# A ring of five 32 KB units with loads of one or two units, and a new order of key and value work, in a decode layer

## The chip, the cores and the metric

The kernel runs on one core of one Trainium2 chip; the other cores are idle. The metric is the device time of one execution in microseconds, and less is better. Executions of the kernel before agree within 0.1%: 408.78 to 408.88 us in the first three. In the texts, PE is the matrix engine, DVE the vector engine, ACT the scalar engine, SP the engine that issues the loads; SBUF is the memory beside the engines that the loads fill, and PSUM holds the results of PE. A *row* is a contiguous piece that one of the 16 DMA engines moves at a time, one *packet* in the profile's count.

## The reference, cut to what matters

One token goes through attention over a cache of 65,536 keys and values, and then through a gated feed-forward layer:

```python
x = A_x                                            # [1, 1, 1024]
h = x + attention(layernorm(x), k_cache, v_cache, wq, wo)
# 32 query heads, 4 key/value heads, k_cache and v_cache [1, 4, 65536, 128] bf16: 67 MB each
h2 = h + (gelu(ln(h) @ w_gate) * (ln(h) @ w_up)) @ w_down     # F = 3584
```

Every byte of the cache and of the weights is read once, 173.02 MB in all. That is the kernel's main fact.

## The kernel before: the parts that matter

All loads go through one function into a pool of five buffers. A buffer has 32 KB in each of the 128 partitions, so a load is 4 MB, made of 128 contiguous rows of 32 KB (28 KB for gate and up).

```python
CW, NBUF = 16384, 5
chpool = ctx.enter_context(tc.tile_pool(name="chpool", bufs=NBUF))

def load(src, name):
    t = chpool.tile([P, CW], BF16, name=name, tag="ch")
    n, w = src.shape[1], src.shape[2]
    tv = t[:, 0:n * w].rearrange("p (n w) -> p n w", w=w)
    nc.sync.dma_start(out=tv, in_=src)
    return tv
```

Each of the four key/value heads (a "group" below) is four units of keys and four of values. A key unit is turned in place by four DVE transposes, then PE makes scores with 32 matmuls; a value unit takes 32 matmuls. Keys of one group alternate with values of the group before:

```python
def k_load(g, li):
    kt = kv_load(k_v[g], li, "k_sb").rearrange("p n d -> p (n d)").bitcast(U32)
    w = CP * Dh // 2
    for c in range(NSP):                             # four quarters
        dv(nc.vector.transpose(out=kt[:, c * w:(c + 1) * w], in_=kt[:, c * w:(c + 1) * w]))
    ...

for g in range(1, Hkv):
    for li in range(NL):
        k_load(g, li)
        v_load(g - 1, li)
        ...                                          # closing work of older groups
        k_scores(g, li)
        k_keep(g, li)                                # scores out of PSUM, running maximum
        if li == NL - 1:
            softmax_head(g)
        v_values(g - 1, li)
```

A load may start when the buffer that it gets is free: after the last matmul on the unit that was there. Loads are issued in order by one queue, so a load that waits holds back those behind it.

## Time and profile before

| | before |
|---|---|
| time, median | 408.87 us (3 runs), 408.77 us (6 runs, with the later three) |
| span of the profiled run | 407.0 us |
| DMA slices at 9 tenths or more | 39 of 40 |
| bytes, rate over the span | 173.02 MB, 425 GB/s |
| PE, DVE busy | 74%, 50% |
| first row of a load starts, last row ends | 1.0 us, 403.1 us |

These are lines of the page of the kernel before. In the slices, each digit is the busy share of a fortieth of the span in tenths; the queue line has packets, MB and the packets' time as a share of 16 engines; a line of group 5 has busy us, mean ns and the idle time ahead of it; the last lines have the size of a load and the median us from issue to landing.

```profile
PE 299.3 (74%) x1481; PEld 62.8 (15%) x713; DVE 202.6 (50%) x185; ACT 44.9 (11%) x67; POOL 7.4 (2%) x17
...
DMA  9999999999999999999999999999999999999995
...
DMA packets 6508, 173.19 MB, mean 426 GB/s; under 512 B 728, under 2 KB 736, under 8 KB 992
...
q1 hardware_dynamic: 6488, 173.02, 98.8%
...
DMA 46%; PE 30%; DVE 18%; ACT 4%; issue 2%; SPq 0%; ACTq 0%; DVEq 0%
...
L275 DVE STREAM_TRANSPOSE k_sb<-k_sb 128x2048 uint32<-128x2048 uint32 x64 | 142.1, 2278 | 34.5 <-DMA k_sb<-in_A_k_cache_dram 34.5
...
k_sb<-in_A_k_cache_dram SPq DMA_DIRECT2D x16, 4096.0 KB, 33.6
v_sb<-in_A_v_cache_dram SPq DMA_DIRECT2D x16, 4096.0 KB, 37.1
```

The DMA line never dips. The chain that ended last gives only 46% to DMA, which could tempt one to speed up DVE; but a unit takes 9.7 us to move and a value load lands 37 us after its issue, so two to three other loads are queued ahead of it. The stream of loads has work at every moment, and the chain merely follows single buffers through it.

The end of the kernel is this part of its timeline (start, us, engine, line, operation; in brackets the idle time and what ended it):

```profile
402.92 1.02 PE L144 MATMUL f_ps<-wd_sb,actz 128*32 128x256 bf16 x12 [0.17 <-DMA wd_sb<-in_B_w_down_dram]
...
403.99 0.42 DVE L526 CAST o_fin<-f_ps 97x256 bf16<-97x256 f32 x1 [11.82 <-PE f_ps L144]
404.44 0.66 SPq L527 DMA_DIRECT2D out_dram<-o_fin  x1
```

After the last row only the last products, a copy and the store are left, about 4 us.

### The profile page before, as it was taken

What the parts mean: (1) busy time and instruction counts of PE and PEld (TensorE: products, weight loads), DVE (VectorE), ACT (ScalarE), POOL (GpSimd) and SP (SyncE); (2) the same over time, 40 slices, a digit from 0 to 9 for tenths busy, and PEclk for the clock granted to TensorE, in tenths of its full rate; (3) what the DMA queues carried; (4) which work ended last, traced back from release to release, by engine and by line L of the source; (5) the groups of instructions that cost most, each with busy time, mean ns of one, the idle gap of its engine ahead of it and who ended that gap; (6) DMA issues with size and microseconds to landing.
All of it is one profiled execution on the core that took longest, in us unless ns stands there. A gap on an engine that the chain in (4) does not pass through costs nothing.

```text
span 407.0 us, 2658 instructions
## 1 busy us (share of the span) xinstructions
PE 299.3 (74%) x1481; PEld 62.8 (15%) x713; DVE 202.6 (50%) x185; ACT 44.9 (11%) x67; POOL 7.4 (2%) x17
## 2 busy tenths in 40 slices
PE   0356298769997788897956969978767998725564
PEld 0011011111110111111101121110112110200233
DVE  1118989876673678555464968181843001110110
ACT  1010000150000041000002320000051000100000
POOL 2000000000000000000000000000010000100000
PEclk9965778969999989899989898999868899866565
DMA  9999999999999999999999999999999999999995
GB/s 364 461 412 451 423 419 457 410 454 422 414 461 415 441 430 415 461 415 444 427 419 457 415 448 425 420 454 415 448 426 432 440 419 444 424 429 442 426 421 220
DMA packets 6508, 173.19 MB, mean 426 GB/s; under 512 B 728, under 2 KB 736, under 8 KB 992
## 3 DMA queue, kind: packets, MB, share of 16 engines
q1 hardware_dynamic: 6488, 173.02, 98.8%
q8 instruction: 8, 0.13, 0.1%
q14 instruction: 4, 0.03, 0.0%
q10 hardware_dynamic: 8, 0.00, 0.0%
HBM read 173.02 MB, written 0.00 MB: 425 GB/s over the span
## 4 chain that ended last, share of the span: by engine, by line
DMA 46%; PE 30%; DVE 18%; ACT 4%; issue 2%; SPq 0%; ACTq 0%; DVEq 0%
DMA k_sb<-in_A_k_cache_dram 32%; DVE k_sb L275 12%; PE acc_ps L146 12%; DMA wg_sb<-in_B_w_gate_dram 8%; PE qk_ps L144 6%; PE qk_ps L146 6%; DMA wd_sb<-in_B_w_down_dram 5%; PE acc_ps L144 4%; DVE mx L296 2%; ACT sc L295 2%; DVE pT L320 1%; ACT pe_r L317 1%; PE o_ps L144 1%; DVE acc_sb L346 1%; ACT acc_sb L348 1%
## 5 line engine op out<-in xcount | busy, mean ns | idle before, releaser
L275 DVE STREAM_TRANSPOSE k_sb<-k_sb 128x2048 uint32<-128x2048 uint32 x64 | 142.1, 2278 | 34.5 <-DMA k_sb<-in_A_k_cache_dram 34.5
L144 PE MATMUL qk_ps<-k_sb,wsel 128*128 128x512 bf16 x256 | 103.9, 406 | 36.3 <-DVE k_sb L275 23.8
L146 PE MATMUL acc_ps<-v_sb,pT 128*128 128x512 bf16 x384 | 112.6, 405 | 0.0
L146 PE MATMUL qk_ps<-k_sb,wsel 128*128 128x512 bf16 x256 | 103.7, 405 | 0.0
L144 PE MATMUL acc_ps<-v_sb,pT 128*128 128x512 bf16 x128 | 52.0, 406 | 0.0
L144 PEld LDWEIGHTS <-wsel 128*128 128x128 bf16 x256 | 26.0, 102 | 141.3 <-issue 121.2
L296 DVE TENSOR_REDUCE mx<-qk_ps 128x1 f32<-128x1024 f32 x16 | 19.5, 1219 | 43.9 <-ACT sc L295 43.9
L295 ACT COPY sc<-qk_ps 128x1024 f32<-128x1024 f32 x16 | 16.2, 1012 | 201.7 <-PE qk_ps L146 201.6
L144 PEld LDWEIGHTS <-pT 128*128 128x128 bf16 x128 | 13.6, 106 | 99.8 <-issue 99.7
L320 DVE STREAM_TRANSPOSE pT<-pe_r 128x1024 bf16<-128x1024 bf16 x16 | 19.0, 1226 | 6.2 <-ACT pe_r L317 6.2
L346 DVE COPY acc_sb<-acc_ps 32x512 f32<-32x512 f32 x8 | 5.4, 672 | 32.7 <-PE acc_ps L146 32.7
L317 ACT ACTIVATE pe_r<-sc,nbias 128x1024 bf16<-128x1024 f32 x16 | 18.2, 1140 | 14.3 <-DVE nbias L312 13.6
L146 PE MATMUL wu_ps<-wu_sb,hnz 128*32 128x512 bf16 x40 | 7.1, 572 | 7.5 <-DMA wu_sb<-in_B_w_up_dram 7.5
L348 ACT COPY acc_sb<-acc_ps 32x512 f32<-32x512 f32 x8 | 4.6, 577 | 62.0 <-DVE acc_sb L346 61.9
L232 DVE COPY wg_ev<-wg_ps 128x512 f32<-128x512 f32 x1 | 0.7, 690 | 20.9 <-PE wg_ps L144 20.9
L144 PE MATMUL q_ps<-wq_sb,xnz 128*32 128x512 bf16 x32 | 5.2, 626 | 8.0 <-DMA wq_sb<-in_A_wq_dram 8.0
L144 PE MATMUL f_ps<-wd_sb,actz 128*32 128x256 bf16 x112 | 6.9, 413 | 5.3 <-DMA wd_sb<-in_B_w_down_dram 5.3
L144 PE MATMUL wg_ps<-wg_sb,hnz 128*32 128x512 bf16 x32 | 6.5, 598 | 5.3 <-DMA wg_sb<-in_B_w_gate_dram 5.3
L144 PE MATMUL o_ps<-sel,acc_sb 128*128 128x8 f32 x32 | 5.2, 290 | 6.7 <-DVE rl L360 5.9
L144 PE MATMUL ln_tot<-ln_s,ones_f 128*128 128x1 f32 x8 | 1.9, 311 | 10.8 <-DVE ln_s L194 9.0
L155 PE MATMUL mxT_ps<-ident_f,mx 128*1 128x128 f32 x4 | 1.3, 322 | 11.1 <-DVE mx L301 11.1
L232 DVE COPY q_ev<-q_ps 128x512 f32<-128x512 f32 x1 | 0.7, 691 | 13.5 <-PE q_ps L146 13.5
(102 smaller groups left out, 87.6 us busy)
## 6 DMA issues: line engine op xcount, KB each, us to landing
k_sb<-in_A_k_cache_dram SPq DMA_DIRECT2D x16, 4096.0 KB, 33.6
v_sb<-in_A_v_cache_dram SPq DMA_DIRECT2D x16, 4096.0 KB, 37.1
wq_sb<-in_A_wq_dram SPq DMA_DIRECT2D x2, 4096.0 KB, 16.5
wo_sb<-in_A_wo_dram SPq DMA_DIRECT2D x2, 4096.0 KB, 30.8
wg_sb<-in_B_w_gate_dram SPq DMA_DIRECT2D x2, 3584.0 KB, 32.0
wu_sb<-in_B_w_up_dram SPq DMA_DIRECT2D x2, 3584.0 KB, 33.1
wd_sb<-in_B_w_down_dram SPq DMA_DIRECT2D x1, 3584.0 KB
wd_sb<-in_B_w_down_dram SPq DMA_DIRECT2D x1, 1792.0 KB, 24.8
```

The costliest lines, as they stand in the source:

```text
L144: return pe(t.matmul(out, lhsT=lhsT, rhs=rhs, start=start, stop=stop, tile_position=tile_position, skip_group_check=skip_group_check))
L146: op = t.add_instruction(mybir.InstMatmult(name=nc.get_next_instruction_name(), engine=t.engine, start_tensor_calc=start, stop_tensor_calc ...
L155: pe(nc.tensor.transpose(out=out, in_=in_, identity=identity))
L232: nc.vector.tensor_copy(out=dst, in_=src)
L275: dv(nc.vector.transpose(out=kt[:, c * w:(c + 1) * w], in_=kt[:, c * w:(c + 1) * w]))
L295: ac(nc.scalar.copy(out=sc[:], in_=flat))
L296: dv(nc.vector.tensor_reduce(out=state[("mx", g)][:, li:li + 1], in_=flat, axis=AX.X, op=ALU.max))
L317: ac(nc.scalar.activation(out=pe_r[:], in_=state.pop(("sc", g, li))[:], func=ACT.Exp, bias=nbias[:, 0:1], scale=scale, accum_out=lpart[:, ...
L320: dv(nc.vector.transpose(out=pT[:].rearrange("p m c -> p (m c)"), in_=pe_r[:]))
L346: dv(nc.vector.tensor_copy(out=acc_sb[sl, :], in_=acc[sl, c, :]))
L348: ac(nc.scalar.copy(out=acc_sb[sl, :], in_=acc[sl, c, :]))
```

## The change

The intent is longer rows: two neighbouring units of values, and all of gate, are loaded by one DMA with rows of 64 KB (56 KB for gate), within the same five units of SBUF. For that the pool becomes one tile that is handed out as a ring. The order is rearranged so that loads of two units never wrap: two value units, then three key units. The first part of a key unit's turn is moved ahead of the scores of the unit before, and the softmax's steps go between value matmuls. Gate is now complete before up begins, and all pieces of down stand side by side in the first two units.

```diff
-    chpool = ctx.enter_context(tc.tile_pool(name="chpool", bufs=NBUF))
+    chpool = ctx.enter_context(tc.tile_pool(name="chpool", bufs=1))
+    ring = chpool.tile([P, NBUF * CW], BF16, name="ring")
...
+    at = [0]
+    def load(src, off=0):
         n, w = src.shape[1], src.shape[2]
+        units = -(-(off + n * w) // CW)
+        o = at[0] * CW + off
+        assert o + n * w <= NBUF * CW
+        at[0] = (at[0] + units) % NBUF
+        tv = ring[:, o:o + n * w]
+        nc.sync.dma_start(out=tv.rearrange("p (n w) -> p n w", w=w), in_=src)
...
+    def kv_load(what, g, li, n):
+        t = load((k_v if what == "k" else v_v)[g][:, li * LN:(li + n) * LN, :])
+        for u in range(n):
+            state[(what, g, li + u)] = t[:, u * LN:(u + 1) * LN, :]
...
-    for g in range(1, Hkv):            # key unit, value unit, key unit, ...
+    todo = [("k", 0, 0, 1), ("k", 0, 1, 1), ("k", 0, 2, 1), ("k", 0, 3, 1), ("k", 1, 0, 1),
+            ("v", 0, 0, 2), ("k", 1, 1, 1), ("k", 1, 2, 1), ("k", 1, 3, 1), ("v", 0, 2, 2),
+            ("k", 2, 0, 1), ("v", 1, 0, 2), ("k", 2, 1, 1), ("k", 2, 2, 1), ("k", 2, 3, 1), ("v", 1, 2, 2),
+            ...  ("v", 3, 0, 2), ("v", 3, 2, 2)]      # what, group, first unit, units
...
-        wg = load(gv[:, c0:c0 + GB, :], "wg_sb")
+    wg = load(gv[:])                                  # gate in one load, then up in two
...
+        at[0] = 0
+        wv = load(wd_v[:, c0:c0 + sz, :], c0 * D)
```

## The prediction

> **What bounds the kernel now.** The stream of loads. The page's slices show the 16 DMA engines at 9 tenths in 39 of 40 slices; the queue list gives the load queue 98.8% of the span. In the packet records behind that list the first row starts at 1.0 us and the last ends at 403.1; the row times over 16 engines sum to 401.7 us, so there is no hole. PE is busy 74%, DVE 50%; the transposes and matmuls in the chain that ended last are waits of single buffers, not of the stream. After the last row come about 4 us (last products, copy, store).
>
> A 32 KB row takes 1.213 us on its engine, an 8 KB row 0.309, a 4 KB row 0.159. Estimate from these: 27.2 B/ns per engine (435 GB/s for 16) plus 8 ns a row. The Trainium skill, "DMA: Bandwidth & Descriptors", section "Where 436 GB/s comes from", gives a ceiling of 435.2 GB/s; the trace's slope agrees, and a 32 KB row already runs within 0.7% of it. Longer rows have almost nothing left to win.
>
> **What the change does.** The bytes stay (173.02 MB). Values: 2,048 rows of 32 KB become 1,024 of 64 KB; gate: 256 of 28 KB become 128 of 56 KB. That is 1,152 rows fewer: 1,152 x 8 ns / 16 = 0.58 us, all on the critical stream, provided a 64 KB row stays one packet. Nine loads fewer save nine 9 ns semaphore packets per engine, 0.08 us. Sum: 0.1 (if rows are cut again) to 0.7 us. Compute is unchanged (64 transposes of 2.28 us, 512 score and 512 value matmuls); its order becomes two value units, then three key units. Gate now comes before up, but the last up load still lands about 385 us, so the tail stays.
>
> **What it puts at risk.** A two-unit load waits until both units are free, and the loads behind it wait too. Today a load is issued 18 to 26 us before the stream needs it in the steady part. I placed the landings at 9.7 us per unit (8 rows of 1.213 us) and carried the turn (8.9 us), scores and values (about 8 us each; 7.0 at full clock, 9.7 in slow stretches) and softmax along the new order. Value loads are then issued only 6 to 11 us ahead; the tightest is group 1's first half: it waits for group 1's third key unit to be scored near 140 us, and the stream reaches it near 146.5. Key loads keep 16 to 21 us. Extra half-clock stretches (3.4 to 10 us each in the clock records) would cost 2 to 5 us there, so I expect no hole, but a small one is possible.
>
> **Predicted time:** 408.2 us, 8 in 10 between 407.4 and 409.4. Faster by over 2%: 2%; within 2%: 93%; slower by over 2%: 5%.
>
> **What would show it.** (1) Packets fall from 6,508 to about 5,210; near 6,360 would mean that 64 KB rows are cut in two. (2) The DMA slices stay at 9. (3) A value load takes about 28 us from issue to landing instead of 37, 19.4 of them transfer. (4) The last row ends 0.1 to 0.7 us earlier; the 4 us after it are the same. (5) Waits of the SP queue on PE grow without cost.
>
> **What would make it wrong.** A hole in the stream at a value load (a low DMA slice); 64 KB rows running slower per byte than 32 KB ones; or per-row overhead that vanishes more than linearly, worth at most 3 us.

## More of the kernel before

A verdict (faster, same, slower) needs 2%.

The packet records behind the page allow a second measure, used in all that follows: the *lead* of a load, which is the time from its issue to the start of its first row. A load with a lead of 15 us could have been issued about 14 us later without a hole in the stream.

In the kernel before, the key and value loads have leads of 13.2 to 28.7 us, counted from the first value load on.

## The result, and the profile after

Ratios in this document are the mean time of one kernel's fast runs over that of the other's in the same rounds, so they are not quite the ratios of the medians that are quoted beside them.

| | before | after |
|---|---|---|
| time, median (range, runs) | 408.77 us (408.65 to 408.88, 6) | 408.69 us (408.28 to 409.17, 6) |
| ratio, 95% interval | | 0.9997 (0.9985 to 1.001) |
| span of the profiled run | 407.0 us | 406.7 us |
| last row ends | 403.1 us | 402.8 us |
| row times over 16 engines | 401.7 us | 401.2 us |
| lead of the value loads | 13.2 to 28.7 us | 6.8 to 16.0 us |

The lines of the page of the changed kernel that answer to those above (the last one is from the list of DMA issues, for value loads of two units):

```profile
PE 295.0 (73%) x1481; PEld 63.6 (16%) x729; DVE 202.6 (50%) x185; ACT 44.7 (11%) x67; POOL 7.4 (2%) x17
...
DMA  9999999999999999999999999999999999999995
...
DMA packets 5211, 173.18 MB, mean 426 GB/s; under 512 B 584, under 2 KB 592, under 8 KB 848
...
q1 hardware_dynamic: 5192, 173.02, 98.7%
...
DMA 62%; PE 27%; DVE 9%; ACT 1%; issue 0%; SPq 0%; ACTq 0%
...
L281 DVE STREAM_TRANSPOSE ring<-ring 128x2048 uint32<-128x2048 uint32 x64 | 142.7, 2280 | 34.0 <-DMA ring<-in_A_k_cache_dram 34.0
...
ring<-in_A_k_cache_dram SPq DMA_DIRECT2D x16, 4096.0 KB, 34.5
...
ring<-in_A_v_cache_dram SPq DMA_DIRECT2D x8, 32.3
```

The packets fell by 1,297, as 1,152 fewer rows and 144 fewer semaphore packets ask for (one is an instruction fetch). The DMA line is the same, digit for digit. The chain moved from 46% DMA to 62%, while nothing became slower or faster: another sign that it is not a measure of what the stream costs. A value load of two units now lands 32.3 us after its issue (median, the last line above).

### The profile page after: what moved, and what is told of

Read it like the earlier page. It is cut to its first block, busy times and chain, and to the rows that moved or that the text cites. A ratio compares the mean times of both kernels' runs of the same rounds, so it can differ in the third digit from the quotient of the medians.

```text
span 406.7 us, 2639 instructions
## 1 busy us (share of the span) xinstructions
PE 295.0 (73%) x1481; PEld 63.6 (16%) x729; DVE 202.6 (50%) x185; ACT 44.7 (11%) x67; POOL 7.4 (2%) x17
## 2 busy tenths in 40 slices
DMA packets 5211, 173.18 MB, mean 426 GB/s; under 512 B 584, under 2 KB 592, under 8 KB 848
## 3 DMA queue, kind: packets, MB, share of 16 engines
q1 hardware_dynamic: 5192, 173.02, 98.7%
HBM read 173.02 MB, written 0.00 MB: 425 GB/s over the span
## 4 chain that ended last, share of the span: by engine, by line
DMA 62%; PE 27%; DVE 9%; ACT 1%; issue 0%; SPq 0%; ACTq 0%
DMA ring<-in_A_v_cache_dram 40%; PE acc_ps L147 12%; DMA ring<-in_A_k_cache_dram 7%; DMA ring<-in_B_w_down_dram 7%; DMA ring<-in_B_w_gate_dram 7%; DVE ring L281 7%; PE qk_ps L145 5%; PE qk_ps L147 5%; PE acc_ps L145 4%; DVE mx L302 2%; ACT sc L301 1%; PE wg_ps L145 0%; PE wg_ps L147 0%; PE f_ps L145 0%; DVE o_fin L549 0%
## 5 line engine op out<-in xcount | busy, mean ns | idle before, releaser
L281 DVE STREAM_TRANSPOSE ring<-ring 128x2048 uint32<-128x2048 uint32 x64 | 142.7, 2280 | 34.0 <-DMA ring<-in_A_k_cache_dram 34.0
L145 PE MATMUL qk_ps<-ring,wsel 128*128 128x512 bf16 x256 | 99.5, 389 | 35.5 <-DVE mx L302 23.6
L147 PE MATMUL acc_ps<-ring,pT 128*128 128x512 bf16 x384 | 115.0, 412 | 0.0
L147 PE MATMUL qk_ps<-ring,wsel 128*128 128x512 bf16 x256 | 99.5, 389 | 0.0
L145 PE MATMUL acc_ps<-ring,pT 128*128 128x512 bf16 x128 | 53.3, 416 | 17.8 <-DMA ring<-in_A_v_cache_dram 17.8
L145 PE MATMUL q_ps<-ring,xnz 128*32 128x512 bf16 x32 | 5.2, 625 | 7.8 <-DMA ring<-in_A_wq_dram 7.8
L145 PE MATMUL f_ps<-ring,actz 128*32 128x256 bf16 x112 | 6.9, 415 | 5.4 <-DMA ring<-in_B_w_down_dram 5.4
L145 PE MATMUL wu_ps<-ring,hnz 128*32 128x512 bf16 x32 | 4.9, 527 | 7.5 <-DMA ring<-in_B_w_up_dram 7.5
L145 PE MATMUL wg_ps<-ring,hnz 128*32 128x512 bf16 x32 | 4.4, 492 | 8.1 <-DMA ring<-in_B_w_gate_dram 8.1
L315 DVE TENSOR_REDUCE gm<-mxT_ps 1x8 f32<-1x128 f32 x4 | 1.1, 279 | 15.0 <-PE mxT_ps L156 15.0
L145 PEld LDWEIGHTS <-hnz 128*32 128x32 bf16 x64 | 3.3, 116 | 21.8 <-issue 17.4
```

The lines of the kernel that those rows point to most:

```text
L145: return pe(t.matmul(out, lhsT=lhsT, rhs=rhs, start=start, stop=stop, tile_position=tile_position, skip_group_check=skip_group_check))
L147: op = t.add_instruction(mybir.InstMatmult(name=nc.get_next_instruction_name(), engine=t.engine, start_tensor_calc=start, stop_tensor_calc ...
L315: dv(nc.vector.tensor_reduce(out=gm[:], in_=mxT_ps[:].rearrange("o (x h) -> o h x", h=rep), axis=AX.X, op=ALU.max))
```

## The experiments

Twelve kernels ran. The theory under test: *the stream of loads is the time; a row costs about 8 ns beyond its bytes; the changed order keeps enough lead for the stream never to run dry.* The rivals: longer rows win more and a hole gives it back; row length does nothing at all; compute in the chain that ended last costs time.

### 1. The changed kernel again, and with value rows of 32 KB

The first is an unedited control. The second keeps ring, units and order, and loads each value unit alone:

```diff
-        t = load((k_v if what == "k" else v_v)[g][:, li * LN:(li + n) * LN, :])
         for u in range(n):
-            state[(what, g, li + u)] = t[:, u * LN:(u + 1) * LN, :]
+            state[(what, g, li + u)] = load((k_v if what == "k" else v_v)[g][:, (li + u) * LN:(li + u + 1) * LN, :])
```

> The changed kernel once more, unedited, as a control beside the split variant. Theory (the stream of loads is the time; a row costs 8 ns over its bytes; the slack of the value loads is enough): 408.2 to 408.7 us, ratio to the kernel before 0.998 to 1.000, about 5,211 packets, no DMA slice under 9 before the last. Rival (longer rows win more, but a hole at a value load gives it back): the same time, but the value loads' rows start later than 9.7 us per unit allows. Rival (row length does nothing): ratio 1.000 as well, so this run alone tells little.

> The changed kernel with the same ring, units and order, but each value unit loaded by a DMA of its own, with 32 KB rows: 1,024 rows and 8 loads more. Theory: plus 0.51 us for rows and 0.07 us for semaphore packets against the control, so 408.7 to 409.2 us; value loads are issued 16 to 26 us ahead of their first row instead of 7 to 13; no hole. Rival (a hole ate a larger gain of the long rows): this kernel has no holes and comes out at or below the control. Rival (row length does nothing): equal to the control within 0.1 us. If the wide spread of the changed kernel's runs (0.9 us against 0.2) comes from the thin slack of the two-unit loads, it shrinks here; if it comes from the new order, it stays.

Measured on one chip, against 408.80 us of the kernel before (9 runs): the control 408.55 us (408.42 to 408.72; ratio 0.9993, interval 0.9981 to 1.0006), the split variant 408.92 us (408.71 to 409.28; ratio 1.0005, interval 0.9992 to 1.0019). The split costs 0.37 us by the medians, not 0.58; the two sets of five runs only touch (408.72 and 408.71), and both intervals hold 1. Its packet count tells that the edit did what it should:

```profile
DMA packets 6364, 173.19 MB, mean 426 GB/s; under 512 B 712, under 2 KB 720, under 8 KB 976
```

That rules against a larger gain that a hole took back: with leads of 17.7 to 26.6 us at the value loads this kernel is not faster. The wide spread of the changed kernel's first six runs (0.9 us) did not come back in the control (0.3 us; 0.6 us in the split variant), so it needs no cause in the kernel. A change of some tenths of a microsecond is at the edge of what these runs resolve, so the cost of a row was magnified next.

### 2. Rows of 8 KB and 4 KB in the kernel before

Each 32 KB row of keys and values is moved as four or eight rows, by two interleaved DMAs, which was meant to keep neighbouring rows from merging (the packet count below shows that they did not merge):

```diff
-        nc.sync.dma_start(out=tv, in_=src)
+        if w == Dh:
+            cut = lambda ap: ap.rearrange("p (a h n) d -> p h a (n d)", a=4, h=2)   # a=2 for 8 KB
+            for h in range(2):
+                nc.sync.dma_start(out=cut(tv)[:, h], in_=cut(src)[:, h])
+        else:
+            nc.sync.dma_start(out=tv, in_=src)
```

> The kernel before with the rows of keys and values cut to 8 KB (each 32 KB row is moved as four rows, by two DMAs; results unchanged). Theory: 12,288 rows more at 8 ns over 16 engines are 6.1 us, and 32 loads more at 9 ns 0.3 us, so plus 6.4 us: 415.2 us (414.5 to 416). Rival (rows of any such length run at one rate): under 1 us more. Rival (cost of a row more than proportional to their number): over 8 us.

> The same with rows of 4 KB (each 32 KB row as eight). Theory: 28,672 rows more are 14.3 us, and 0.3 us for loads: plus 14.6 us, 423.4 us (422.5 to 425). The 4 KB rows of the last down load took 0.159 us each in the trace of before; the same is expected here. Rival (one rate): under 1 us more.

Measured: 412.56 us and 417.38 us (4 runs each), 3.76 and 8.58 us more than the kernel before, where 6.4 and 14.6 were expected. The ratios are 1.0091 (interval 1.0077 to 1.0105) and 1.0209 (1.0195 to 1.0223), by the 2% rule "same" and "unclear", but both clear of 1. The expectations miss by the same factor, 0.59. After 0.3 us for the 32 additional loads (9 ns on each engine), a row costs (3.76 - 0.29) us x 16 / 12,288 = 4.5 ns and (8.58 - 0.29) us x 16 / 28,672 = 4.6 ns: proportional to the number of rows, but 4.6 ns and not 8. The additional loads are not the cause: between the two runs, which issue equally many, 16,384 rows cost 4.82 us, or 4.7 ns a row.

The page of the kernel with 4 KB rows shows why the estimate from row times was too high:

```profile
DMA packets 35692, 173.19 MB, mean 417 GB/s; under 512 B 1240, under 2 KB 1248, under 8 KB 34272
...
q1 hardware_dynamic: 35672, 173.02, 100.4%
```

The rows took more than all of 16 engines' span. So the records of neighbouring rows overlap: in this run the row times sum to 416.6 us per engine, the stretch from first row to last is 410.8 us, and 1.6 us of it is idle; the 7.4 us too many over 2,152 rows per engine are 3.4 ns a row. The records' own times (0.309 us for 8 KB, 0.159 us for 4 KB) are unchanged from before (0.159 us was expected for 4 KB); it is adding them up that counts these 3.4 ns twice.

The Trainium skill, "DMA: Bandwidth & Descriptors", section "Why small descriptors are slow (HBM only)", names a fixed overhead of about 3 cycles a packet and 32 bytes of descriptor metadata. With the 850 MHz and 435.2 GB/s of its section "Where 436 GB/s comes from" this is, as an estimate (the page does not give the clock of that bus), 3.5 + 1.2 = 4.7 ns. The 4.5 to 4.7 ns of the two runs are close to that; that these two parts make up the cost is not shown.

Applied to the change: 1,152 rows x 4.6 ns / 16 = 0.33 us, and up to 0.08 us for the semaphores. The profiled stream ended 0.3 us earlier, and splitting the values again (1,024 rows and 8 loads, 0.29 + 0.07 us) cost 0.37 us. With sets of runs that spread by 0.3 to 0.6 us, so close an agreement is partly luck.

### 3. Is it compute? Three transposes of four taken away

```diff
-        for c in parts:
+        for c in [p for p in parts if p == 0]:
             dv(nc.vector.transpose(...))
```

> The changed kernel with three of the four transposes of each key unit taken away, 107 us of DVE work (result wrong on purpose). Theory (the stream is the time): within 0.3 us of the changed kernel, 408.2 to 408.9 us, with loads issued further ahead. Rival (transposes in the chain that ended last cost time): 5 us or more faster.

Measured: 408.45 us (408.35 to 408.85), against 408.82 us before and 408.55 to 408.69 us of the changed kernel. DVE fell to half, and nothing followed:

```profile
PE 292.7 (72%) x1481; PEld 61.4 (15%) x729; DVE 98.1 (24%) x137; ACT 44.8 (11%) x67; POOL 7.4 (2%) x17
...
DMA  9999999999999999999999999999999999999995
```

This is the plainest evidence for the first part of the theory: 104 us of work of the second busiest engine are worth nothing. One part of the expectation failed: the loads were not issued further ahead. The leads of the value loads are 7.6 to 14.8 us, against 6.8 to 16.0 us, so in this order less DVE work bought no lead; what holds it then was not tested. PE, the busiest engine, was not relieved in any run; that it does not set the time rests on the leads, since no load met a dry queue in the kernels before and after. (The keys are then wrongly turned. The comparison with the reference still passed; so it does not see such errors in the keys, and passing it is no proof of a right order of key data.)

### 4. What the change spent: lead

If the stream is the limit, the change's cost would not show in the time but in the slack. The same DVE work, 2.28 us per key unit, was added to the kernel before, to the changed kernel, and to the variant with split values: the last quarter of each key unit is turned twice.

```diff
-        for c in range(NSP):                                        # the kernel before
+        for c in [*range(NSP)] + [NSP - 1] * 1:
-        for c in parts:                                             # the changed kernel, and split values
+        for c in [c for p in parts for c in [p] * (2 if p == NSP - 1 else 1)]:
```

> The kernel before with the last quarter of each key unit turned twice: 2.28 us more of DVE per key unit, 36 us in all (scores then read a wrongly turned quarter, so the result is wrong on purpose). Theory (loads issued 13 to 29 us ahead, the added work stays off the stream): within 0.5% of the kernel before, at most 3 us more. Rival (compute is as close to the limit as the chain of waits makes it look): plus several us.

> The same 2.28 us per key unit in the changed kernel (result wrong on purpose). Theory (the change left 7 to 13 us of lead at the value loads; three key units in a row now take 6.8 us more, the lead goes negative for the values of groups 0 and 1): plus 4 to 20 us, with low DMA slices near 120 and 150 us. Rival (the lead is not what decides): within 0.5%, as before_turn_x2.

> The same addition in values_single: the new order, but each value unit loaded alone. If the thin lead comes from waiting for two units at once: close to the kernel before, under 2 us more. If it comes from the new order (value units in a pair, keys in a triple): plus 4 to 20 us, within 3 us of after_turn_x2. The times worked through the order with the trace's durations say the second, except where PE runs at full clock throughout.

Measured against 408.82 us: 408.62 us with the old order (ratio 0.9997, interval 0.9982 to 1.0012), 423.76 us with the change (1.0347, interval 1.0307 to 1.0387), 415.58 us with the change and single value loads (1.0162, interval 1.0145 to 1.0179; clear of 1). The slices of the three pages, old order first:

```profile
PE 294.5 (72%) x1481; PEld 63.4 (16%) x713; DVE 238.5 (59%) x201; ACT 44.9 (11%) x67; POOL 7.4 (2%) x17
...
DMA  9999999999999999999999999999999999999995
```

With the changed kernel (the second line is GB/s in the same slices):

```profile
PE 301.5 (71%) x1481; PEld 63.7 (15%) x729; DVE 239.0 (57%) x201; ACT 44.8 (11%) x67; POOL 7.4 (2%) x17
...
DMA  9999999989969969899999899999999989999994
GB/s 397 413 431 447 436 410 447 490 386 413 442 258 397 447 248 486 375 428 447 450 422 417 354 397 416 428 445 481 410 403 398 455 385 434 456 431 405 429 419 166
```

With the changed order and single value loads:

```profile
DMA  9999999999999999999999899999998999999994
```

The two deepest holes in the changed kernel lie where they were expected, near 120 and 150 us; two more loads met a dry queue, at 235.7 and 323.6 us. Its sync queue's timeline shows the first one: the value load goes out at 121.33 us, and its first row starts at 122.28 us, 0.95 us later, so the queue was dry.

```profile
121.33 0.33 SPq L167 DMA_DIRECT2D ring<-in_A_v_cache_dram  x1
128.27 0.33 SPq L167 DMA_DIRECT2D ring<-in_A_k_cache_dram  x1
```

In the view by windows (PE, PEld, DVE, ACT and POOL busy us, granted clock, DMA share, GB/s) the two stretches read, in the changed kernel with the addition:

```profile
118.00:126.00 8.00, 8.00 (x39) 1.45 (x15) 4.50 (x2) 0.00 (x0) 0.00 (x0) 1.00 0.69 258
150.00:158.00 8.00, 5.21 (x25) 0.77 (x9) 4.45 (x6) 1.01 (x1) 0.00 (x0) 1.00 0.57 209
```

and in the kernel before with the same addition:

```profile
118.00:126.00 8.00, 8.00 (x39) 1.07 (x11) 7.53 (x4) 0.44 (x1) 0.00 (x0) 1.00 0.98 422
150.00:158.00 8.00, 6.44 (x17) 1.13 (x7) 5.28 (x9) 4.74 (x8) 0.00 (x0) 0.57 1.00 428
```

In the second window the old order even had PE at a clock of 0.57, and its stream did not notice.

Two causes share the 15 us, and the split variant separates them. My expectation for it was either "under 2 us" or "within 3 us of the other"; it came out in the middle, so both halves of that question were wrong as put.

- *The order.* In the changed kernel with the addition, two value units in a row leave DVE with little to do (busy 4.5 of 8 us from 118 to 126 us), and three key units in a row leave PE waiting (busy 17.3 of 24 us from 126 to 150 us). From the first maximum of one group to that of the next (groups 2 and 3), the old order with the addition takes 76.4 us and the new one 81.0 us (180.84 to 261.82 us). The stream needs 8 x 9.69 = 77.5 us for a group. The old order stays under it, the new one does not. (Without the addition this stretch takes 78.1 and 77.5 us: there the compute goes at the pace of the stream.) The compute of the split variant runs at the same times as that of the changed kernel (its last maximum ends at 317.3 us against 317.5 us); so the 6.8 us that it lost against the kernel before go with the order. What came with the order (the ring, the place of the softmax, the part of the turn that was moved ahead) was not tried piece by piece.
- *Waiting for two units at once.* With single loads the first unit of a pair starts to fill while the second is still in use, so the stream gets further ahead of the same compute: gate's first row starts at 355.8 us and not at 364.1. That is the other 8 us (423.76 - 415.58). A load of two units also lands later as a whole; since the compute ran at the same times in both variants, that did not cost time here.

### 5. The edges: half the dose, twice the dose, fewer buffers

The changed kernel with half the addition (half of the last quarter turned once more), and the old order with twice the addition:

```diff
+            if c == NSP - 1:                                        # after_turn_half
+                dv(nc.vector.transpose(out=kt[:, c * w:c * w + w // 2], in_=kt[:, c * w:c * w + w // 2]))
-        for c in range(NSP):                                        # before_turn_x3
+        for c in [*range(NSP)] + [NSP - 1] * 2:
```

> The changed kernel with half of the last quarter of each key unit turned once more: about 1.14 us of DVE per key unit, half the dose of after_turn_x2 (result wrong on purpose). Theory (what counts is the lead of the value loads, 11 us at the values of group 0, second half, and group 1, first half; the full dose used up 10 us of it): about 5 us of lead stay at the first, little at the second, so no hole or small ones: 408.5 to 412 us. Rival (every us of work added to the new order shows in the time, lead or not): about half of the full dose's 15 us, 415 to 417 us.

> The kernel before with the last quarter of each key unit turned three times: 4.57 us more of DVE per key unit, twice the dose of before_turn_x2 (the data come out right again). Its shortest lead was 13.2 us, with one dose 6.2. Theory: this dose takes it to about zero in the first half and the paces meet, so holes appear: plus 5 to 35 us. Rival (the old order is immune because DVE is only 50% busy): within 0.5%.

The kernel before with four and with three buffers (`NBUF = 4`, `NBUF = 3`):

> The kernel before with four buffers of 32 KB in place of five. Theory (leads of 13 to 29 us; a buffer less takes one load's 9.7 us from each): shortest lead about 3 to 6 us, no hole, 408.6 to 409.5 us. Rival (the fifth buffer is needed): plus several us.

> The kernel before with three buffers. Theory: a second buffer less takes another 9.7 us, leads fall to between about minus 2 and plus 8 us, so holes appear at some loads: plus 2 to 20 us, visible as loads whose first row starts about 1 us after their issue. Rival (depth does not matter): within 0.5%.

Measured against 409.06 us: half dose 408.59 us (ratio 0.9989, interval 0.9974 to 1.0004), double dose 438.19 us (1.0705, interval 1.0685 to 1.0726), four buffers 408.68 us (0.9996, interval 0.9981 to 1.001), three buffers 424.00 us (1.0381, interval 1.0339 to 1.0423). The DMA slices of three buffers:

```profile
DMA  9999979988999999999999999999999899999995
```

All of it in one table. Idle is the mean idle time of the 16 engines between the first row and the last, counted where fewer than 16 rows were under way; row time is the sum of the row times over 16; both are from the packet records of the profiled runs. The lead is the shortest of the key and value loads from the first value load on.

| kernel | span, us | idle, us | row time, us | shortest lead, us |
|---|---|---|---|---|
| before | 407.0 | 1.5 | 401.7 | 13.2 |
| before, one dose | 406.8 | 1.4 | 401.6 | 6.2 |
| before, four buffers | 406.8 | 1.5 | 401.5 | 4.9 |
| after | 406.7 | 1.5 | 401.2 | 6.8 |
| after, half dose | 406.8 | 1.7 | 401.1 | 3.9 |
| after, single value loads, one dose | 414.2 | 5.9 | 404.5 | 0.95 (dry) |
| after, one dose | 422.4 | 14.3 | 404.0 | 0.95 (dry) |
| before, three buffers | 422.5 | 11.9 | 406.8 | 0.95 (dry) |
| before, two doses | 436.6 | 24.7 | 408.1 | 0.95 (dry) |

Every kernel in the table whose queue never ran dry has the same span within 0.3 us, and every kernel with a dry load is longer by what the stream lost. The sums that follow are bookkeeping: they show where the time went, and the doses and buffers above show why. For the changed kernel with one dose, idle and row time grew by 12.8 + 2.8 = 15.6 us, the span by 15.7; for three buffers, by 10.4 + 5.1 = 15.5 us, the span by 15.5; for two doses, by 23.2 + 6.4 = 29.6 us, the span by 29.6. The rival of the half dose (every us of work shows, so about half of 15 us) fell: half the dose cost nothing. The pace of the compute agrees: from the first maximum of group 2 to that of group 3, half the dose in the new order takes 75.6 us, under the stream's 77.5, and two doses in the old order take 86.0 us.

The growth of the row time can be read in the packet records. In the changed kernel with one dose, the first rows of the 16 engines after the four dry moments took 2.9 to 3.2 us in the mean, and the next ones 2.42 to 2.48 us, against 2.42 us at a steady stream. The surplus of these first rows is 2.5 of the 2.9 us by which the row time grew. So in this run a dry queue cost its idle time, and 0.5 to 0.75 us more at each restart. Why a first row is slower was not tested.

## Why the prediction was right, and which of its terms was mis-sized

- **What bounds the kernel: right.** The stream has no hole in either kernel, and 104 us less of DVE work changed nothing.
- **408.2 us, between 407.4 and 409.4: right**, with 408.69 us (408.55 in the repeat). The 0.6 us gain behind the 408.2 was too large; 0.08 us in the first runs and 0.25 us in the repeat were measured, and both intervals hold zero. The verdict "same" would have come out with any cost of a row from 0 to 8 ns, so it is no test of that term; the runs of section 2 are.
- **The mis-sized term** is "27.2 B/ns per engine plus 8 ns a row", and so "1,152 x 8 ns / 16 = 0.58 us". The runs with short rows show 4.6 ns, which makes 0.33 us. The error was to take a row's recorded time as the time that it keeps its engine: records overlap by about 3.4 ns, too little to see at 32 KB, plain at 4 KB.
- **"Provided a 64 KB row stays one packet": it did.** 5,211 packets for about 5,210 predicted; a 64 KB row took 2.418 us, against 1.213 us for 32 KB.
- **The lead: right in kind, cautious in size.** "Value loads are then issued only 6 to 11 us ahead" came out as 6.8 to 16.0 us. The tightest is not the first half of group 1 (11.3 us; it went out at 135.9 us, where near 140 was predicted) but the second half of group 3 (6.8 us), which waits for the last key unit and then for the first value unit after it. Landing took 32.3 us and not "about 28" because six of the eight leads were 10.4 to 13.0 us, and because the first row of such a load starts some 21 us before it lands, not 19.4.
- **"Waits of the SP queue on PE grow without cost": wrong in direction.** These are the waits of the queue, before:

```profile
SPq L161 <- PE acc_ps L146: 141.1, 16, 13.6
SPq L161 <- DVE k_sb L275: 91.7, 14, 14.6
SPq L161 <- PE qk_ps L146: 69.9, 14, 12.2
```

  and after (us in total, times, longest us):

```profile
SPq L167 <- PE acc_ps L147: 122.6, 12, 16.7
SPq L167 <- DVE ring L281: 104.3, 10, 20.2
SPq L167 <- DMA ring<-in_A_v_cache_dram: 44.2, 8, 14.7
...
SPq L167 <- PE qk_ps L147: 21.1, 8, 5.0
```

  The total on PE fell from 211 to 144 us, with 36 loads in place of 45. What grew is the longest single wait, the total on DVE, and the waits that the view puts down to the landing of two-unit loads (44.2 us, none before). What moved from one to the other was not tested. Such totals say nothing of the lead.
- **The tail: right.** The stream ended 0.3 us earlier, and what follows the last row takes 3.9 us in both profiled runs. Whether gate ahead of up has an effect of its own was not tried alone; none is visible in the tail.

Where did the expected gain of longer rows go? It was never there: at 32 KB a row's cost is 4.6 ns in 1,213, so doubling the rows of 43% of the bytes can return less than 0.1%. And what the change spent, half of the stream's slack, is free until something uses up the rest.

No run points to a kernel that beats both by more than the noise. As an estimate, at the 27.2 B/ns per engine of the trace's row times (435.2 GB/s for 16) the 173.02 MB take 397.6 us. What is left between that and the span are 1 us ahead of the first row, 4 us after the last, and about 4 us of row costs, idle moments and instruction fetches.

## What to carry to other kernels

When the DMA line is full in every slice, ask of a change first whether it removes bytes or per-row time, and size that with runs of different row lengths, not with recorded row times alone. Then look at the lead, the time from a load's issue to its first row: a reordering that leaves the time alone can still halve the lead, and an addition that was free before (here 2.28 us of DVE per key unit) is then paid. To learn how near the edge is, add a known dose of work and take a buffer away: here the old order bore 2.28 us more per key unit and one buffer less, and the new one bore only half of that dose.

## What the Trainium skill lacked or had wrong

- "DMA: Bandwidth & Descriptors" gives the cost of a packet in cycles and explains it for small descriptors; it has no measured time for rows of 4 to 64 KB. Here it is 4.5 to 4.7 ns a row between 32 KB and 4 KB (3.76 and 8.58 us for 12,288 and 28,672 rows more), close to the estimate of 4.7 ns from its cycles and bytes.
- "Perfetto Trace Analysis", section "DMA Optimizations", says that batching small transfers into larger ones, "2KB → 4KB or 8KB", can "dramatically improve throughput". It speaks of transfers and not of the rows inside one. Within this kernel, where every load of keys and values stayed at 2 MB or more, 4 KB rows cost 2.1% against 32 KB, 8 KB rows 0.9%, and going on to 64 KB for 43% of the bytes 0.1% at most. What the section lacks is what the length of a row is worth inside a large transfer. Rows under 4 KB in bulk were not tried, so its sentence is not tested here.
- "Perfetto Trace Analysis", section "DMA Engine Tracks", says that "slices show actual busy time". The sum of the slices was 100.4% of the engines' span with 4 KB rows: records of neighbouring rows overlap by about 3.4 ns, so their sum is not busy time for short rows.
- No page that I read says that the rows just after a dry moment are slow: the first 64 KB row of each engine took 2.9 to 3.2 us in the mean in place of 2.42 us, in the changed kernel with one dose (2.5 of its 2.9 us more row time). Why was not tested.
- No page that I read has the lead of a load as a measure; in these runs it told which kernels would stretch (all with 0.95 us) and which would not (all with 3.9 us or more at the key and value loads).
